# Chunked linear attention into a cosine-gated MLP on one core: pair loading for six chunks instead of four, and two chunks of a pair on two row tiles

## Chip, cores, metric

One core of a Trainium2 chip. The metric is the device time of one execution in microseconds; lower is better.

## What is computed

Per batch (4) and head (8), over 768 time steps with head size 48, a state of 48x48 decays per row and takes up k v^T; the output is q times the state. The outputs of all heads (3072 x 384) go through an MLP with h * cos(h) between two matmuls.

```python
for t in range(S):
    state = alpha[:, :, t, :, None] * state + np.einsum('bhd,bhe->bhde', k[:, :, t], v[:, :, t])
    y[:, :, t] = np.einsum('bhd,bhde->bhe', q[:, :, t], state)
x = y.transpose(0, 2, 1, 3).reshape(B * S, H * D)
h = x @ w_in                      # 384 -> 2048
out = (h * np.cos(h)) @ w_out     # 2048 -> 384
```

## The kernel before

Time is cut into 24 chunks of 128 rows, six for each batch; chunks 2g and 2g+1 are pair g. Within a chunk the recurrence is matrix work: the logarithms of alpha are summed from the chunk's start by a triangular matmul, k is divided and q multiplied by the exponentials of the sums, and then scores (k q), a causal mask, scores times v, and the state of the chunk before times q give the outputs. The state is carried from chunk to chunk with its decay.

For the first SG pairs (two before) a load brings two neighbouring time rows of a head together, 384 bytes in a run instead of 192: partition p holds rows 2p and 2p+1 of the 256 rows of the pair. A buffer then holds the even rows, another the odd rows, of both chunks, the first chunk on partitions 0 to 63 and the second on 64 to 127. Sums, masks and matmuls have forms of their own for that (`sup`, or `j // 2 < SG`).

The order of all work is written out in the string ORDER. Each word is a letter for a unit and a number of a chunk, a pair or a part; the units are issued in this order, each onto its engine's queue, and every engine works its queue strictly in that order. The letters:

- a k q v: loads on SP's queue (L192 to L202). w0 w1: halves of the first MLP matrix, w2 w3: of the second, from POOL's queue (L204 to L214). D: transpose by DMA, o: store of 128 rows, both on SP.
- l: logarithm (ACT, L226), C: sums (TensorE, L234 to L249), E: exponentials (ACT, L255 and L256).
- K and B: k scaled on POOL or DVE (L260); R and O: q scaled on POOL or DVE (L266); P: v cast (POOL, L270); M: decay factors (POOL, L274).
- T, t: transposes on TensorE and their copy (DVE, L286). A, m: scores and mask (L300 or L306, DVE L311). S, u, b: state, its sum with the state before (DVE, L346, or L336 for a first chunk) and its decay (POOL, L336).
- Y, y: outputs of one chunk and their copy out of PSUM (DVE, L406); Q, z: the same for a pair (L385, DVE L425).
- H, h, g: 4 of 16 column blocks of the first MLP matmul for a pair (24 matmuls, L445), its cosine (ACT, L453), the gate (DVE, L458). H0 to H3 belong to pair 0, H4 to H7 to pair 1. H4i and H4i+1 use w0, the others w1. V, e: a quarter of the second MLP matmul of a chunk (4 matmuls, L468; V0 to V3 is chunk 0, the first two quarters use w2, the others w3), and the copy of the finished rows (ACT, L472).
- x: dummy matmuls on a zeroed tile (L481), as many as the number says.

PSUM is handed out by `Slots`: three slots `two` of two banks (for C, A, Q, H) and two slots `one` of one bank (for T, S, Y and the rows of V). A slot that is given back (by E, m, z, g, t, u, y, e) goes to the unit that next takes one in ORDER, which then waits for that reader. SBUF buffers go round by number: four of alpha, three each of k, q and v pairs.

## Time and profile before

| | us |
|---|---|
| median of 5 runs (181.39 to 181.69) | 181.41 |
| the profiled execution | 181.39 |
| its span, first to last instruction | 179.62 |
| what lies around the span (difference) | 1.77 |
| TensorE busy in the span | 172.0 |
| DVE, ACT, POOL busy | 121.8, 111.5, 78.4 |
| end of the last matmul | 175.80 |
| copy of the last rows on ACT (L472) | 0.49 |

The span runs from the first to the last instruction of the program; times in the views count from its start. An engine's busy time is the union of its instructions' times. "idle before" names how long an engine stood before an instruction, and what released it. The chain of waits goes back from the last instruction, at each step to what released it or to the instruction ahead of it on its engine. q1 is the DMA queue of SP, q0 that of POOL; a queue's share is the time that its packets took over that of 16 engines, which passes 100% where an engine has more than one packet under way.

### The profile page before, as it was taken

The page shows a single profiled execution, that of the slowest core. Times are in us where ns is not written, and L with a number is a line of the kernel's source. Part 1 is how long each engine was busy: PE and PEld are TensorE (multiplying, and loading weights), DVE is VectorE, ACT ScalarE, POOL GpSimd, SP SyncE. Part 2 cuts the span into 40 slices and gives each one's busy share as a digit, 9 for nine tenths or more (in the row PEclk, how much of TensorE's full clock was granted, in tenths as well). Part 3 has the DMA queues.
Part 4 walks back from the last instruction along what each step waited for, and adds up shares of the span by engine and source line. Part 5 has one row for each costly group of instructions (what it writes and reads, how often), then busy time and mean ns, then how long its engine had stood idle before and what let it go on. Part 6 is the DMA issues. An engine that isn't in the chain of part 4 may idle for free.

```text
span 179.6 us, 5251 instructions
## 1 busy us (share of the span) xinstructions
PE 172.0 (96%) x2227; PEld 125.9 (70%) x2227; DVE 121.8 (68%) x152; ACT 111.5 (62%) x124; POOL 78.4 (44%) x133
## 2 busy tenths in 40 slices
PE   7978799999999999999999999999999999999991
PEld 2455688866787587876787866875788757788660
DVE  6178898957359688465987596368787679755620
ACT  3544345864778598866869895797765521455431
POOL 7259710223689127952129337952187804100100
PEclk9999999999999999999999999999999999999999
DMA  6999999999999997999999999999819993010112
GB/s 157 325 293 178 199 191 185 186 190 218 215 212 134 204 235 169 198 143 207 222 219 205 222 212 190 158 259 236 190 47 219 211 115 135 0 43 6 46 44 88
DMA packets 113719, 31.01 MB, mean 173 GB/s; under 512 B 107808, under 2 KB 112928, under 8 KB 113696
## 3 DMA queue, kind: packets, MB, share of 16 engines
q1 hardware_dynamic: 110816, 27.53, 75.4%
q0 software_dynamic: 2880, 3.15, 10.7%
q8 instruction: 17, 0.28, 0.6%
q14 instruction: 6, 0.05, 0.1%
HBM read 25.17 MB, written 4.72 MB: 166 GB/s over the span
## 4 chain that ended last, share of the span: by engine, by line
PE 87%; SPq 4%; DMA 3%; DVE 2%; POOL 2%; issue 1%; ACT 0%; POOLq 0%
PE one L468 36%; PE two L445 35%; PE two L385 5%; SPq L197 3%; PE two L306 3%; DMA k_sb<-in_k_dram 3%; PE one L331 2%; PE two L245 2%; PE one L281 2%; PE one L385 1%; PE two L247 1%; DVE qkT L286 1%; SPq L201 1%; POOL kqb L260 1%; POOL vpb L270 1%
## 5 line engine op out<-in xcount | busy, mean ns | idle before, releaser
L458 DVE TENSOR_TENSOR g_sb<-two,c_sb 128x1024 bf16<-128x1024 f32 x48 | 58.2, 1221 | 26.1 <-ACT c_sb L453 25.4
L453 ACT ACTIVATE c_sb<-two,halfpi 128x1024 bf16<-128x1024 f32 x48 | 52.8, 1113 | 32.5 <-PE two L445 30.9
L468 PE MATMUL one<-w,g_sb 128*128 128x384 bf16 x384 | 69.7, 326 | 0.0
L445 PE MATMUL two<-xT,w 128*128 128x256 bf16 x576 | 68.3, 273 | 0.0
L445 PEld LDWEIGHTS <-w 128*128 128x128 bf16 x576 | 55.1, 98 | 8.2
L468 PEld LDWEIGHTS <-g_sb 128*128 128x128 bf16 x384 | 35.9, 98 | 20.9
L260 POOL TENSOR_TENSOR kqb<-k_sb,icp 128x384 bf16<-128x384 f32 x21 | 20.9, 1000 | 26.2 <-DMA k_sb<-in_k_dram 13.6
L336 POOL TENSOR_TENSOR ub<-sc,Em 128x384 bf16<-128x384 f32 x20 | 16.6, 830 | 34.3 <-DVE sc L346 34.2
L311 DVE TENSOR_TENSOR A_sb<-two,mask_f 128x1024 bf16<-128x1024 f32 x20 | 23.5, 1217 | 2.6 <-PE two L306 2.5
L270 POOL CAST vpb<-v_sb 128x384 bf16<-128x384 f32 x24 | 12.2, 514 | 24.3 <-DMA v_sb<-in_v_dram 24.3
L266 POOL TENSOR_TENSOR kqb<-q_sb,cp 128x384 bf16<-128x384 f32 x20 | 19.9, 1000 | 6.0 <-DMA q_sb<-in_q_dram 4.8
L472 ACT ACTIVATE o_sb<-one 128x384 f32<-128x384 f32 x24 | 11.7, 489 | 16.1 <-PE one L468 15.3
L255 ACT ACTIVATE icp<-two 128x768 f32<-128x768 f32 x12 | 9.7, 810 | 11.7 <-PE two L247 8.3
L425 DVE CAST xT<-two 128x768 bf16<-128x768 f32 x10 | 9.6, 956 | 6.2 <-PE two L385 6.2
L346 DVE TENSOR_TENSOR sc<-one,ub 128x384 f32<-128x384 f32 x20 | 11.0, 551 | 3.7 <-PE one L331 3.6
L226 ACT ACTIVATE lnab<-a_sb 128x768 bf16<-128x768 f32 x12 | 10.1, 844 | 3.5 <-DMA a_sb<-in_alpha_dram 2.2
L481 PE MATMUL one<-warm 128*128 128x512 bf16 x31 | 9.6, 452 | 2.4 <-DVE warm L106 1.2
L220 ACT ACT_TABLE_LOAD x8 | 10.3, 1283 | 0.9 <-PEq L510 0.7
L451 ACT ACT_TABLE_LOAD x8 | 10.3, 1283 | 0.1
L286 DVE COPY qkT<-one 128x1024 bf16<-128x1024 bf16 x9 | 6.1, 687 | 5.8 <-PE one L281 3.5
L256 ACT ACTIVATE cp<-two 128x776 f32<-128x776 f32 x12 | 9.7, 812 | 0.0
L385 PEld LDWEIGHTS <-vpb 128*32 128x32 bf16 (+1 forms) x448 | 8.9, 95 | 1.1 <-issue 0.7
(65 smaller groups left out, 120.8 us busy)
## 6 DMA issues: line engine op xcount, KB each, us to landing
out_dram<-o_sb SPq DMA_DIRECT2D x24, 192.0 KB, 2.9
a_sb<-in_alpha_dram SPq DMA_DIRECT2D x20, 192.0 KB, 3.9
k_sb<-in_k_dram SPq DMA_DIRECT2D x20, 192.0 KB, 3.9
q_sb<-in_q_dram SPq DMA_DIRECT2D x20, 192.0 KB, 4.0
v_sb<-in_v_dram SPq DMA_DIRECT2D x20, 192.0 KB, 3.8
w<-in_moe_w_in_dram POOLq DMA_DIRECT2D x2, 768.0 KB, 9.1
w<-in_moe_w_out_dram POOLq DMA_DIRECT2D x2, 768.0 KB, 15.3
a_sb<-in_alpha_dram SPq DMA_DIRECT2D x2, 384.0 KB, 4.1
```

Source lines behind the costliest of these rows:

```text
L260: eng.tensor_tensor(out=kqb[j % 4][:, 0, :, 0:D], in0=slot(k_t, j), in1=icp_t[j // 2 % 3][:, j % 2].rearrange("s (h d) -> s h d", h=H), op ...
L266: eng.tensor_tensor(out=kqb[j % 4][:, 1, :, 0:D], in0=slot(q_t, j), in1=cp.rearrange("s (h d) -> s h d", h=H), op=ALU.mult)
L270: nc.gpsimd.tensor_copy(out=vpb[j % 4][:, :, 0:D], in_=slot(v_t, j))
L311: nc.vector.tensor_tensor(out=A_t[j % 4].rearrange("s (h t) -> s h t", h=H), in0=two[("A", j)].rearrange("s (h t) -> s h t", h=H), in1=(ma ...
L336: eng.tensor_tensor(out=ub[j % 3][:, :, 0:96].rearrange("r p (a e) -> r p a e", a=2), in0=src.rearrange("r p (a e) -> r p a e", a=2), in1= ...
L346: nc.vector.tensor_tensor(out=sc_t[j % 3], in0=t, in1=ub[(j - 1) % 3][:, :, 0:96], op=ALU.add)
L385: nc.tensor.matmul(t[32 * c : 32 * c + 32, kt * C : (kt + 1) * C], lhsT, rhs, start=start, stop=stop, skip_group_check=True)
L445: nc.tensor.matmul(t[:, m * n : (m + 1) * n], w1[:, kk, f * C : (f + 1) * C], x_t[g % 3][:, kk, bs].rearrange("r b t -> r (b t)"), start=( ...
L453: nc.scalar.activation(out=c_s.take((name, i)), in_=two[(name, i)], func=AF.Sin, bias=halfpi, scale=1.0)
L458: nc.vector.tensor_tensor(out=g_t[g % 3][:, fs, bs], in0=shaped(two[(name, i)], name), in1=shaped(c_s[(name, i)], name), op=ALU.mult)
L468: nc.tensor.matmul(one[("o", j)][:, 0:DM], g_t[j // 2 % 3][:, f, j % 2], w2[:, f], start=(f == 0), stop=(f == NF - 1))
L472: nc.scalar.activation(out=o_s.take(j), in_=one[("o", j)][:, 0:DM], func=AF.Copy)
```

## The change

Three pairs instead of two are loaded in the paired form (SG = 3), so that all six chunks of the first batch are. The decay sums of a paired pair are formed by matmuls of two columns for both chunks at once, and their exponentials are taken by an instruction of their own. A new unit N makes the states of both chunks of a pair: its matmuls alternate between partitions 0 to 63 and 64 to 127, and write two PSUM slots. The outputs of a paired pair are always made for both chunks together by Q, again with alternating halves; the unit Y is not used any more. A new unit n copies the last 128 rows out of PSUM half on ACT and half on DVE. ORDER is written anew throughout. Of its 30 rows, the first six and the last of each are shown.

```diff
--- before.py
+++ after.py
@@ -15,32 +15,32 @@
 
 
 ORDER = """
-a0 l0 x9 C0 E0 q0 k0 a2 O0 O1 B1 l1 v0 v2 a5 x10 C1 K0 P0 P3 M1 k2 x1 T1 a4 E1 q2 T0 t0 t1 x6 A0
-K3 A1 w0 M0 P1 P2 B2 m0 m1 l2 R3 x4 S1 S0 u0 k4 q4 u1 C2 Y1 O2 E2 a7 k5 a6 q5 Y0 y1 x1 T2 w1 y0 w2
-b1 R4 M2 S2 t2 T3 u2 t3 S3 A2 B4 b2 A3 H1 v4 w3 v5 T4 a9 a8 v6 k6 q6 q7 m3 m2 h1 u3 v7 t4 H0 h0 Y3
-Y2 g1 H2 M3 h2 H3 h3 y2 g0 y3 g2 H6 h6 g3 g6 K5 H5 k8 k7 M4 q8 H4 h5 H7 V4 V5 V0 h4 V1 h7 P4 b3 l3
-V2 V3 V6 V7 e0 g5 g4 g7 O5 T5 e1 t5 C3 E3 V8 S4 u4 A4 A5 b4 P5 V9 V10 R6 K6 V11 V12 e2 l4 m5 m4 o2
-o0 Q2 z2 C4 S5 V13 k9 q9 M6 P6 M5 K7 u5 R7 P7 M7 H9 T6 V14 E4 h9 V15 a11 a12 t6 S6 H8 e3 g9 b5 u6
...
-u23 h47 g46 V92 V88 V93 g47 o19 o20 o21 V94 V89 V95 V90 e23 o23 V91 e22 b23 o22
+a0 l0 k0 x9 C0 v0 a2 q0 E0 K0 B1 P0 P1 l1 M0 v2 q2 k2 O0 x14 N0 R1 P2 C1 E1 a4 w0 u0 a7 q4 k4 u1
+M1 K2 w1 l2 R3 T0 t0 T1 t1 O2 w2 P3 b1 w3 M2 x4 A1 A0 T2 C2 m1 m0 B3 Q0 t2 E2 T3 a6 a8 t3 a9 z0 x3
+A3 A2 N1 H1 m3 u2 m2 h1 M4 b2 H0 Q1 u3 h0 g1 z1 g0 R5 R4 K5 M3 H3 K4 b3 H2 h3 g3 h2 H6 h6 H4 g2 g6
+V4 H5 H7 V0 V5 V1 v4 v7 q7 h4 h7 h5 g4 g7 g5 V2 V6 P4 P5 V3 e0 V7 e1 o0 T5 V8 V9 t5 T4 V10 t4 V11
+k6 q6 v6 k7 a10 l3 e2 l4 A4 A5 N2 m4 C3 C4 u4 P7 m5 V12 b4 V13 E3 Q2 M6 R6 E4 V14 B6 u5 P6 R7 z2
+a12 k9 q9 B7 o2 D6 V15 S6 H8 u6 e3 h8 S7 a11 q8 K9 M7 R9 T7 u7 H10 k8 D9 k10 a13 h10 g8 H9 k11 v9
...
+V93 o19 V91 V94 V95 b23 e22 o22 n23 o23
 """
 
 
@@ -88,7 +88,7 @@
 
 
 
-    SG = 2
+    SG = 3
     HC = C // 2
 
     sb = ctx.enter_context(tc.tile_pool(name="sb", bufs=1))
@@ -233,12 +233,11 @@
                 for ii in range(2):
                     nc.tensor.matmul(t[:, i, 0:HD], strict2 if ii > i else incl2,
                                      l[:, ii, :, 0:D], start=(ii == 0), stop=(ii == 1))
-            for c in range(2):
-                for p in range(NP):
-                    for i in range(2):
-                        nc.tensor.matmul(t[:, c, HD + p : HD + p + 1],
-                                         l[:, i, 2 * p : 2 * p + 2].rearrange("s h d -> s (h d)"),
-                                         halves[:, c : c + 1], start=(i == 0), stop=(i == 1))
+            for p in range(NP):
+                for i in range(2):
+                    nc.tensor.matmul(t[:, 0, HD + 2 * p : HD + 2 * p + 2],
+                                     l[:, i, 2 * p : 2 * p + 2].rearrange("s h d -> s (h d)"),
+                                     halves, start=(i == 0), stop=(i == 1))
             return
         for i in range(n):
             l = lnab[j // 2 % 2][:, (j + i) % 2]
@@ -253,7 +252,13 @@
         t = two[("c", j)].rearrange("s (i x) -> s i x", i=2)
         g, s = j // 2 % 3, slice(j % 2, j % 2 + n)
         nc.scalar.activation(out=icp_t[g][:, s], in_=t[:, 0:n, 0:HD], func=AF.Exp, scale=-1.0)
-        nc.scalar.activation(out=cp_t[g][:, s], in_=t[:, 0:n, 0:CW], func=AF.Exp, scale=1.0)
+        if j // 2 < SG:
+            nc.scalar.activation(out=cp_t[g][:, s, 0:HD], in_=t[:, 0:n, 0:HD], func=AF.Exp, scale=1.0)
+            nc.scalar.activation(out=cp_t[g][:, s, HD:CW],
+                                 in_=t[:, 0, HD : HD + 2 * NP].rearrange("r (p c) -> r c p", c=2),
+                                 func=AF.Exp, scale=1.0)
+        else:
+            nc.scalar.activation(out=cp_t[g][:, s], in_=t[:, 0:n, 0:CW], func=AF.Exp, scale=1.0)
         two.give(("c", j))
 
     def scale_k(eng, j):
@@ -317,20 +322,23 @@
 
     def state(j):
         t = one.take(("S", j))
-        if j // 2 < SG:
-            r = slice(HC * (j % 2), HC * (j % 2) + HC)
-            for p in range(NP):
-                for i in range(2):
-                    b = (j // 2 * 2 + i) % 4
-                    nc.tensor.matmul(t[:, p * 96 : (p + 1) * 96],
-                                     kqb[b][r, 0, 2 * p : 2 * p + 2].rearrange("s h d -> s (h d)"),
-                                     vpb[b][r, 2 * p : 2 * p + 2, 0:D],
-                                     start=(i == 0), stop=(i == 1))
-            return
         for p in range(NP):
             nc.tensor.matmul(t[:, p * 96 : (p + 1) * 96],
                              kqb[j % 4][:, 0, 2 * p : 2 * p + 2].rearrange("s h d -> s (h d)"),
                              vpb[j % 4][:, 2 * p : 2 * p + 2, 0:D], start=True, stop=True)
+
+
+    def states(g):
+        t = [one.take(("S", 2 * g + c)) for c in range(2)]
+        for p in range(NP):
+            for i in range(2):
+                b = (2 * g + i) % 4
+                for c in range(2):
+                    r = slice(HC * c, HC * c + HC)
+                    nc.tensor.matmul(t[c][:, p * 96 : (p + 1) * 96],
+                                     kqb[b][r, 0, 2 * p : 2 * p + 2].rearrange("s h d -> s (h d)"),
+                                     vpb[b][r, 2 * p : 2 * p + 2, 0:D],
+                                     start=(i == 0), stop=(i == 1), skip_group_check=True)
 
     def decayed(eng, j, src):
         eng.tensor_tensor(
@@ -349,7 +357,7 @@
 
 
 
-    def outputs(j, t):
+    def outputs(j):
         U = ub[(j - 1) % 3].rearrange("r p e -> r (p e)")
         sup = j // 2 < SG
 
@@ -377,14 +385,6 @@
                                 A_t[b][s, ACOL[h] * C : (ACOL[h] + 1) * C]))
             return mms
 
-        def issue(streams):
-            for i in range(max(map(len, streams))):
-                for c, stream in enumerate(streams):
-                    if i < len(stream):
-                        kt, lhsT, rhs, start, stop = stream[i]
-                        nc.tensor.matmul(t[32 * c : 32 * c + 32, kt * C : (kt + 1) * C], lhsT, rhs,
-                                         start=start, stop=stop, skip_group_check=True)
-
 
 
         states, rest = [[] for _ in range(4)], [[] for _ in range(4)]
@@ -393,26 +393,36 @@
             for x, mm in enumerate(a + b):
                 m = (g // 4,) + mm + (g < 4 and x == 0, x == len(a + b) - 1)
                 (states if sup and x < len(a) else rest)[g % 4].append(m)
-        if sup:
-            issue(states)
-        issue(rest)
+        return states, rest
+
+    def issue(*lists):
+        for i in range(max(len(stream) for _, streams in lists for stream in streams)):
+            for c in range(4):
+                for t, streams in lists:
+                    if i < len(streams[c]):
+                        kt, lhsT, rhs, start, stop = streams[c][i]
+                        nc.tensor.matmul(t[32 * c : 32 * c + 32, kt * C : (kt + 1) * C], lhsT, rhs,
+                                         start=start, stop=stop, skip_group_check=True)
 
     def outputs_one(j):
-        outputs(j, one.take(("y", j)))
+        issue((one.take(("y", j)), outputs(j)[1]))
 
     def ev_outputs_one(j):
-        x, t = x_t[j // 2 % 3][:, :, j % 2], one[("y", j)][:, 0 : 3 * C]
-        if j // 2 < SG:
-            nc.vector.tensor_copy(out=x.rearrange("r k (p i) -> r k i p", i=2),
-                                  in_=t.rearrange("r (k i p) -> r k i p", k=3, i=2))
-        else:
-            nc.vector.tensor_copy(out=x, in_=t.rearrange("r (k t) -> r k t", k=3))
+        nc.vector.tensor_copy(out=x_t[j // 2 % 3][:, :, j % 2],
+                              in_=one[("y", j)][:, 0 : 3 * C].rearrange("r (k t) -> r k t", k=3))
         one.give(("y", j))
 
     def outputs_two(g):
         t = two.take(("y", g))
-        for i in range(2):
-            outputs(2 * g + i, t[:, 512 * i : 512 * (i + 1)])
+        t = [t[:, 512 * i : 512 * (i + 1)] for i in range(2)]
+        states, rest = zip(*(outputs(2 * g + i) for i in range(2)))
+
+        if g < SG:
+            issue(*zip(t, states))
+            issue(*zip(t, rest))
+        else:
+            for x in zip(t, rest):
+                issue(x)
 
     def ev_outputs_two(g):
         t = two[("y", g)].rearrange("r (b x) -> r b x", b=2)[:, :, 0 : 3 * C]
@@ -472,6 +482,13 @@
         nc.scalar.activation(out=o_s.take(j), in_=one[("o", j)][:, 0:DM], func=AF.Copy)
         one.give(("o", j))
 
+
+    def ev_last(j):
+        o, n = o_s.take(j), DM // 2
+        nc.scalar.activation(out=o[:, 0:n], in_=one[("o", j)][:, 0:n], func=AF.Copy)
+        nc.vector.tensor_copy(out=o[:, n:DM], in_=one[("o", j)][:, n:DM])
+        one.give(("o", j))
+
     def store(j):
         nc.sync.dma_start(out=out[j * C : (j + 1) * C, :], in_=o_s[j])
         o_s.give(j)
@@ -486,12 +503,12 @@
         "K": lambda j: scale_k(nc.gpsimd, j), "B": lambda j: scale_k(nc.vector, j), "R": lambda j: scale_q(nc.gpsimd, j), "O": lambda j: scale_q(nc.vector, j),
         "P": cast_v, "M": decay,
         "T": transposes, "t": ev_transposes, "D": dma_transposes,
-        "S": state, "u": ev_state, "b": lambda j: decayed(nc.gpsimd, j, sc_t[j % 3]),
+        "S": state, "N": states, "u": ev_state, "b": lambda j: decayed(nc.gpsimd, j, sc_t[j % 3]),
         "A": scores, "m": mask_scores,
         "Y": outputs_one, "y": ev_outputs_one, "Q": outputs_two, "z": ev_outputs_two,
         "F": lambda i: first("F", i), "f": lambda i: act("F", i), "p": lambda i: gate("F", i),
         "H": lambda i: first("H", i), "h": lambda i: act("H", i), "g": lambda i: gate("H", i),
-        "V": second, "e": ev_second, "o": store, "x": warmup,
+        "V": second, "e": ev_second, "n": ev_last, "o": store, "x": warmup,
     }
     for u in ORDER.split():
         units[u[0]](int(u[1:]))
```

## Prediction

> **What bounds the kernel now.** I read four views, in this order: the page's busy shares, TensorE's waits, the chain of waits over the first 23 us, and the DMA queues in three windows.
>
> ```profile
> PE 172.0 (96%) x2227; PEld 125.9 (70%) x2227; DVE 121.8 (68%) x152; ACT 111.5 (62%) x124; POOL 78.4 (44%) x133
> ```
>
> TensorE is busy for 172.0 of 179.6 us, but 9.6 us of that are the 31 dummy matmuls of L481. All that it waits for is this:
>
> ```profile
> PE one L481 <- DVE warm L106: 1.2, 1, 1.2
> PE one L481 <- DVE qkT L286: 0.8, 1, 0.8
> PE one L385 <- DVE ub L336: 0.6, 1, 0.6
> PE one L481 <- DVE xT L406: 0.4, 1, 0.4
> PE two L300 <- DVE qkT L286: 0.3, 1, 0.3
> ```
>
> Every one lies before 22 us. In the timeline TensorE stands at H1 (the first MLP matmul) at 22.4 us and then runs without a gap to 175.8 us. So the end is the time of H1, plus the TensorE work queued from there, plus 3.8 us of tail (175.84 to 179.62). A change gains by an earlier start, less work after it, or a shorter tail, and loses by any wait behind H1.
>
> What sets the start is in the chain:
>
> ```profile
> 6.55 1.15 SPq L201
> 7.75 4.62 DMA k_sb<-in_k_dram
> 12.49 1.00 POOL kqb L260
> 13.50 0.86 POOL w L208
> ...
> 22.48 0.54 PE two L445 x4
> ```
>
> SP issues one load per 1.19 us; the eighth (k of chunks 2 and 3) lands at 12.36; K3 waits for it on POOL, and behind K3 in POOL's queue stands w0, the first weight DMA. The DMA queues (packets, MB, share of 16 engines) in 2.4 to 9.4, 17 to 25 and 25.5 to 35.5 us:
>
> ```profile
> q1 hardware_dynamic: 5915, 2.24, 115.7%
> ```
> ```profile
> q0 software_dynamic: 711, 1.40, 93.6%
> q1 hardware_dynamic: 848, 0.16, 17.3%
> ```
> ```profile
> q0 software_dynamic: 1918, 1.46, 92.9%
> q1 hardware_dynamic: 1922, 0.36, 33.5%
> ```
>
> Before the weights come, q1 (SP's loads) alone fills the engines: 845 packets per us, and a load is 1024 packets whether of one chunk or of two, so about 1.2 us each. Once the weights (q0) flow, the two queues take turns packet by packet, and SP's loads fall to 106, then 192 packets per us. The weight stream is one unbroken run: first packet 15.11 us (1.68 us after w0's issue began at 13.43), last at 36.93. Its four DMAs land at 21.67, 26.32, 32.27 and 37.25; their users H1, H2, V4 and V2 run at 22.4, about 27.3 or later, 35.1 and 37.7. The cover is only 0.5 to 0.8 us for the first and the last. An earlier H1 alone is therefore worth less than 1 us: the weights would be late next.
>
> **What the Trainium skill says.** "DMA: Bandwidth & Descriptors", Specifications: transfers reach line rate from 512 B on. The trace agrees in effect: 384 B packets go at 845 per us, 192 B ones (9.5 to 12 us, 2734 in 2.5 us) at 1094, so twice the bytes cost 1.3 times the time. Its section on queues, rings and completion order: an engine goes round robin over its queues at packet granularity; 1918 against 1922 packets above is that. "TensorEngine Tiling (Array Packing)", Key Properties and Gotcha 1: tiles of different rows run in parallel, a change of mode drains the array, and two row tiles can't use one PSUM bank at once. No row of before shows two row tiles of these matmuls together, but the mode drain is there: four V matmuls take 0.65 us, and 0.76 behind a tiled group. "TensorE: Matmul & The Clock Gate", Part 1: an idle window of about 3.4 us halves the clock; the trace shows 1.00 throughout, with 1.2 us as the longest wait.
>
> **The change, part by part** (durations from the timeline's starts).
> - *TensorE work.* States: 16 matmuls of L325 for two chunks take 0.63 us, 40 ns each; N does the same 16 on two row tiles in two banks: 8 x 42 = 0.34, saving 0.3 per pair if they overlap, 0 if not. Outputs: Y3 and Y2 take 4 streams of 12 (0.28) and 32 (0.56) matmuls twice, 1.68 us; Q1 needs 24 on full rows (6 x 55 ns) and 64 on eight tiles (8 x 55 ns) plus two drains of 0.1: about 0.97, so -0.7 (bounds -0.8 and 0). Column sums: 8 instead of 16 of 25 ns for the first two pairs (-0.2 each). The third pair's cumulative sum takes 4 instead of 2 of 163 ns: +0.33; its scores, states and outputs cost the same as plain ones. Of all this only Q1 and (as before) what follows lies behind H1. Dummies: 30 instead of 31.
> - *ACT and DVE.* Three exps of 128x8 more, about 0.2 each, and one PSUM copy becomes two of 0.53 for the third pair. Both engines wait for TensorE at that place, so I cost them at nothing; uncovered they are 0.8 us.
> - *Loads.* The third pair's four tensors take four DMAs of 1024 packets instead of eight: 4 x 1.2 = 4.8 us less DMA time before 40 us. SP has four issues less.
> - *Order of loads and of w0.* This is what counts. SP now issues a0 k0 v0 a2 q0 v2 q2 k2 a4. At 1.19 us per load they land at 4.15, 5.34, 6.5, 7.8, 9.0, 10.2, 11.4, 12.5, 13.7. On POOL w0 now stands behind K0 P0 P1 M0 R1 P2 and not behind K3. Walk: C0 ends 0.2 sooner, icp 6.7 to 7.5; K0 7.7 to 8.65 (0.95 each); P0, P1 to 9.6; M0 9.75; R1 to 10.7; P2 (v2 has landed) to 11.15; w0 issues at 11.15 instead of 13.43, 2.3 us sooner. w1 (behind K2), w2 and w3 come at about 13.5, 15.3 and 17.6, well before the stream needs them. So the stream shifts by 2.3 us: landings 19.4, 24.0, 30.0 and 35.0; q4 and k4, now 384 B packets, are in its turns and cost it some 5 ns per packet, 0.3 us by w2's end: 30.3 and 35.4.
> - *TensorE's walk.* N0 at 9.65 (P1), C1 to 10.9, T0 and T1 to 11.8, A1 and A0 12.8 to 13.3 (t1 on DVE), C2 when a4 and l2 are done: a4's last packet is due at 13.0, just as the stream starts (11.15 + 1.68 = 12.8), so I give it 0.8 us of delay: landing 14.5, C2 15.4 to 16.3. m0 ends 15.65; Q0 16.3 to 17.0; T3, t3 18.3, z0 19.35; N1 is done by then. H1 at 19.45, against w0 at 19.4. H0, Q1 (m2 22.2) to 23.1; H3 waits for w1 to 24.0; H3 H2 H6 H4 take 5.2; V4 waits from 29.3 for w2, 30.3; V4 H5 H7 V0 V5 V1 take 0.65 + 2.6 + 1.95 = 5.2; V2 at 35.5. Before, V2 stood at 37.75 with the same units done: a lead of 2.25 us. It is set by the weights: row-tile savings, the exps, and up to 1 us of delay of a4 are hidden in the two waits of 0.9 and 1.0 us, and no wait is long enough for the clock.
> - *Behind V2.* Loads after the stream: k4 lands at 35.3, v4 at about 39.1, P5 40.1; T5 at 38, T4 at 39.8 and N2 at 42.4 find them. New here: V7 T5 V8, where before C3 stood between T5 and V8; V8's bank is given back by e1 0.65 us after V7's end, T5 covers 0.45: 0.25 us lost. N2 takes both banks at once and waits for e2, 0.1 to 0.2. C4 and V12 queue behind it. Further on the number of changes between plain and tiled groups is 39 in both orders; I allow 0.1 for waits.
> - *Tail.* ACT's 0.49 us copy of the last rows becomes two halves side by side; ACT's rows of 384 and 1024 elements (0.49, 1.11) give 0.30 for 192, DVE about 0.35. SP's store waits for the later: -0.14.
>
> Sum: -2.25 + 0.25 + 0.15 + 0.1 - 0.14 = -1.9 to -2.0. The profiled execution took 181.39 us (span 179.62 and 1.77 around it), the median is 181.41: 179.4.
>
> **Rivals.**
> - *Given back (180.5).* The loads behind the stream come later than I walk them; K5, P5 or b4 stall TensorE between 36 and 47 us by 1 us more. For: m4, u4, b4, Q2 follow each other with 0.1 us of slack. Against: DMA has 4.8 us less to do.
> - *Hidden anyway (181.3).* The row tiles don't overlap and mode drains grow: by the walk that is +1.4 us ahead of H3, almost all within the waits for weights; by itself it makes no more than 0.5. It needs a later stall too.
> - *Slower (185).* The weights overtake a4. a4's last packet is due at 13.04, w0's first at 12.8. Before, q1 got some 260 to 330 packets through in the stream's first 0.5 us, then nearly none for 1 us, then 87 per us. If w0 starts at 12.0, 900 packets are left, some 640 are trapped for 7.4 us, a4 lands near 22, C2 holds back Q0 behind it, H1 is at 27 and V2 at 41: +3.5. It decides once a4 lands after 19.2, about 400 trapped packets. Against: P2 can't run before v2 lands at 10.2, so w0's first packet isn't before 12.5.
>
> **How the numbers follow.** The forecast (gain 1.4 to 2.9) has 0.62; given back (0.4 to 1.4) 0.13; a gain over 2.9 (the stream itself shorter, by fewer competing packets) 0.05; no difference 0.08; slower 0.12. 0.2% is 0.36 us, about what a measurement of this kernel can tell. Faster 0.80, same 0.08, slower 0.12. Low 178.3 (3.1 gained), high 181.3: these leave out slower and most of no change.
>
> **What would show it.** Right: w0's issue near 11.2 us and landing near 19.4, waits of TensorE for w before H3 and V4, V2 near 35.5. Wrong: a wait of ACT's ln for a_sb beyond 16 us, TensorE waits over 0.5 us behind 40 us, or w landing as before.

## The result, and the profile after

| | before | after |
|---|---|---|
| median, us (executions) | 181.6 (78) | 182.66 (41) |
| the profiled execution | 181.39 | 182.28 |
| its span | 179.62 | 180.32 |

Time after over time before is 1.0033, with a 95% interval of 1.0016 to 1.005: slower by a third of a per cent, where 179.4 us was forecast. Ratios and means compare undisturbed executions with those of the kernel before; the medians hold all of them, and in experiments 2 and 9 most were disturbed.

A part of this lies outside the span. What lies around the span was 1.77 us in the profiled execution before and 1.96 in the one after. In the 42 listed executions of the changed kernel it is 1.7 to 3.1 (median 2.05); in 191 of the kernel before, run beside the experiments, 1.72 to 1.85. The mean span is 180.35 against 180.14, the mean of what lies around it 2.09 against 1.78: about 0.3 of the 0.6 us that the ratio stands for, and the two profiled executions, 0.70 apart, overstate the difference of the spans. The lost clock told of below does not set the two kernels apart: 7 of 42 and 29 of 191 executions have a mean clock of 0.991 or less.

The two spans are cut at three events that both have: H1 (the first MLP matmul), V2 (the first user of w3) and the end of the last matmul, in the two profiled executions. Of each stretch the view gives its bounds, its length, busy time and instructions of each engine, TensorE's clock, and the DMA share and rate. Before:

```profile
0.00:22.41 22.41, 18.65 (x285) 10.82 (x286) 14.63 (x43) 9.54 (x11) 14.93 (x37) 1.00 1.04 230
22.41:37.73 15.32, 15.32 (x215) 12.56 (x209) 14.09 (x14) 10.17 (x9) 1.67 (x4) 1.00 1.22 191
37.73:175.80 138.07, 138.07 (x1736) 102.52 (x1733) 93.08 (x95) 91.30 (x104) 61.85 (x93) 1.00 0.82 163
175.80:179.62 3.82, 0.01 (x1) 0.00 (x0) 0.00 (x0) 0.49 (x1) 0.00 (x0) 1.00 0.28 103
```

After:

```profile
0.00:20.04 20.04, 17.07 (x270) 9.52 (x271) 13.36 (x41) 9.84 (x14) 14.93 (x37) 1.00 1.02 247
20.04:36.59 16.55, 14.47 (x205) 11.74 (x201) 11.56 (x13) 8.43 (x8) 5.68 (x7) 1.00 1.20 202
36.59:175.96 139.37, 139.32 (x1799) 103.27 (x1797) 95.83 (x100) 93.17 (x105) 59.72 (x90) 1.00 0.78 160
175.96:180.32 4.36, 0.00 (x0) 0.00 (x0) 0.36 (x1) 0.33 (x1) 0.00 (x0) 0.82 0.25 90
```

Stretch by stretch: -2.37, +1.23, +1.30, +0.54, together +0.70. H1 did move forward. Half of that is lost before V2, although TensorE has 0.85 us less to do there (14.47 against 15.32): 2.08 us of the stretch are idle. The rest, and more, is lost to more TensorE work behind V2 and to a longer tail. (V2 is found by counting: the stretch of V matmuls that starts at 34.64 has twelve of 163 ns ahead of it; before, sixteen from 35.13.)

TensorE's waits after:

```profile
PE two L404 <- issue: 2.1, 1, 2.1
PE one L498 <- DVE warm L106: 1.2, 1, 1.2
PE two L234 <- ACT lnab L226: 0.6, 2, 0.4
PE one L286 <- POOL kqb L265: 0.5, 1, 0.5
PE two L305 <- issue: 0.4, 1, 0.4
```

No wait for weights is among them, though two of about 1 us were forecast. The largest is new: "issue", so no engine and no transfer that the view knows released it. It stands in the middle of Q1, between the 33rd and 34th of its 64 score matmuls (timeline of TensorE):

```profile
20.04 2.79 PE L455 MATMUL two<-xT,w 128*128 128x256 bf16 x24
22.77 0.53 PE L404 MATMUL two<-qkT,ub 128*32 128x128 bf16 x24
23.23 0.47 PE L404 MATMUL two<-A_sb,vpb 64*32 64x128 bf16 x33
25.77 0.41 PE L404 MATMUL two<-A_sb,vpb 64*32 64x128 bf16 x31 [2.08 <-issue]
26.12 5.42 PE L455 MATMUL two<-xT,w 128*128 128x256 bf16 x48
```

What ran just ahead of 25.77 on the DMA queues is a packet of q8, the queue that carries the program itself (q8's traffic within the span is 17 packets, 0.28 MB, so 16 KB each). In 23.5 to 24.5 us:

```profile
q0 software_dynamic: 165, 0.13, 80.8%
q1 hardware_dynamic: 165, 0.06, 36.0%
q8 instruction: 1, 0.02, 5.9%
```

This packet ran from 23.54 to 24.48, and TensorE went on 1.3 us later. The Trainium skill ("Runtime: NRT & Kernel Launch", Instruction fetch mechanics) says that an engine's program is refilled in blocks of 16 KiB, 256 instructions, by a DMA queue of its own, and calls the cost mostly hidden. The size agrees with the trace (4,536 matmuls and weight loads make 17.7 such blocks); "hidden" does not.

The places of the holes say the same. Of TensorE's matmuls and weight loads, in order of their starts, 446 stand ahead of the 0.4 us hole in A3, and 702 ahead of the hole in Q1: 256 more. The traces of the changed kernel and of eleven experiments have 18 such holes of 0.38 us or more, ahead of H1 and in Q1. They stand behind 444 or 446 and behind 700 or 702 instructions (some records are missing), 256 apart in all six traces with both, whatever unit is at that place; and each ends 1.2 to 1.5 us after the end of a packet of q8.

Taken as the starts of blocks, which is inferred, these places show how the hole comes about. TensorE works off the block that begins at 19.03 by 23.69, in 4.7 us. The packet of the next block starts 4.5 us after 19.03, takes 0.94, and TensorE goes on 1.3 later: 25.77. Before, at the same place of the count, the block takes from 19.1 to 26.15, 7.0 us, and the packet, 3.0 us after its start, ends 3.1 us ahead of the need. So the hole comes as much from the shorter time that the new forms and order need for 256 instructions as from a later packet. (Further on, packets come up to 3 us ahead of starts counted in this way, so the count serves only up to Q1.)

The weights, landing times in us:

| | w0 | w1 | w2 | w3 | w0 to w3 |
|---|---|---|---|---|---|
| before | 21.67 | 26.32 | 32.27 | 37.25 | 15.58 |
| after | 19.67 | 24.07 | 30.65 | 36.19 | 16.52 |
| forecast | 19.4 | 24.0 | 30.3 | 35.4 | 16.0 |

The lead of 2.0 us shrinks to 1.06. The queues in 25.5 to 28.5 us, before:

```profile
q0 software_dynamic: 573, 0.44, 93.6%
q1 hardware_dynamic: 567, 0.11, 33.2%
```

After:

```profile
q0 software_dynamic: 528, 0.41, 86.1%
q1 hardware_dynamic: 529, 0.20, 38.9%
```

The queues still take turns, packet for packet, but q1's packets are now the pairs' 384 bytes, and the weights (q0) get 8% fewer turns in the same time.

One correction to the text ahead: a unit H has 12 matmuls (four blocks of three), with 12 weight loads, not 24 matmuls.

### The profile page after: what moved, and what is told of

It is laid out like the page before. It is cut to its first block, busy times and chain, and to the rows that moved or that the text cites. A ratio compares the mean times of both kernels' runs of the same rounds, so it can differ in the third digit from the quotient of the medians.

```text
span 180.3 us, 5337 instructions
## 1 busy us (share of the span) xinstructions
PE 170.9 (95%) x2268; PEld 124.5 (69%) x2268; DVE 121.1 (67%) x153; ACT 111.8 (62%) x127; POOL 80.3 (45%) x134
## 4 chain that ended last, share of the span: by engine, by line
PE 87%; SPq 5%; DMA 3%; issue 2%; ACT 1%; DVE 1%; ACTq 0%
PE one L478 35%; PE two L455 35%; PE two L404 6%; SPq L197 5%; PE two L311 3%; DMA a_sb<-in_alpha_dram 3%; PE one L326 2%; PE two L244 2%; PE one L286 2%; PE two L305 1%; PE two L246 1%; PE one L338 1%; ACT lnab L226 0%; PE two L234 0%; DVE qkT L291 0%
## 5 line engine op out<-in xcount | busy, mean ns | idle before, releaser
L271 POOL TENSOR_TENSOR kqb<-q_sb,cp 128x384 bf16<-128x384 f32 x22 | 22.2, 1016 | 17.9 <-DMA q_sb<-in_q_dram 13.6
L316 DVE TENSOR_TENSOR A_sb<-two,mask_f 128x1024 bf16<-128x1024 f32 x18 | 21.3, 1216 | 1.4 <-PE two L311 1.4
L482 ACT ACTIVATE o_sb<-one 128x384 f32<-128x384 f32 x23 | 11.2, 489 | 13.4 <-PE one L478 11.7
L435 DVE CAST xT<-two 128x768 bf16<-128x768 f32 x9 | 8.6, 958 | 5.4 <-PE two L404 5.4
L404 PE MATMUL two<-A_sb,vpb 128*32 128x128 bf16 (+1 forms) x480 | 10.1, 220 | 2.1 <-issue 2.1
L404 PEld LDWEIGHTS <-vpb 128*32 128x32 bf16 (+1 forms) x480 | 8.2, 94 | 3.2 <-issue 2.8
L498 PE MATMUL one<-warm 128*128 128x512 bf16 x30 | 8.8, 447 | 1.4 <-DVE warm L106 1.2
```

The costliest lines, as they stand in the source:

```text
L271: eng.tensor_tensor(out=kqb[j % 4][:, 1, :, 0:D], in0=slot(q_t, j), in1=cp.rearrange("s (h d) -> s h d", h=H), op=ALU.mult)
L316: nc.vector.tensor_tensor(out=A_t[j % 4].rearrange("s (h t) -> s h t", h=H), in0=two[("A", j)].rearrange("s (h t) -> s h t", h=H), in1=(ma ...
L404: nc.tensor.matmul(t[32 * c : 32 * c + 32, kt * C : (kt + 1) * C], lhsT, rhs, start=start, stop=stop, skip_group_check=True)
L482: nc.scalar.activation(out=o_s.take(j), in_=one[("o", j)][:, 0:DM], func=AF.Copy)
```

## Experiments

All ratios are to the kernel before, also where an expectation speaks of the changed kernel, whose own ratio is 1.0033.

Two theories stood after the result. A: the weight stream sets the start, and pair packets slowed it. B: TensorE's own chain sets it, through the hole in Q1. For the time behind V2, the third pair's forms and the tail were suspected.

**1. The weights later.**

```diff
-k2 O0 x14 N0 R1 P2 C1 E1 a4 w0 u0 a7 q4 k4 u1
-M1 K2 w1 l2 R3
+k2 O0 x14 N0 R1 P2 C1 E1 a4 u0 a7 q4 k4 u1
+M1 K2 w0 w1 l2 R3
```

> The changed kernel with w0 behind K2 on POOL, as the kernel before had it behind K3. Theory: the weight stream sets V2. w0 issues near 14.0 instead of 11.2, its first packet at 15.7; w3 lands near 38.5 instead of 36.2, V2 stands there, 2 us later, and the time rises by 1.6 to 2.2 us. Rival: TensorE's own chain (a4, C2, Q0, z0) sets V2, and then less than 0.7 us is lost; a4 lands sooner, near 13.8.

Median 185.04 (four executions), ratio 1.017 [1.0123, 1.0217]; span 183.9. w0 landed at 23.04, w3 at 38.13, V2 stood at 40.19. Waits of TensorE:

```profile
PE two L455 <- DMA w<-in_moe_w_in_dram: 3.5, 1, 3.5
```

So the early place of w0 is needed. But the loss is more than the shift, and V2 came 2.06 us behind w3: in the two windows of 3.41 us behind that wait TensorE's clock was halved (column before the last two):

```profile
18.72:22.13 3.41, 0.89 (x48) 0.65 (x36) 3.41 (x6) 0.17 (x1) 2.32 (x6) 1.00 1.13 202
22.13:25.54 3.41, 2.45 (x12) 1.77 (x13) 0.46 (x1) 0.00 (x0) 3.41 (x5) 0.50 1.12 200
25.54:28.96 3.42, 3.42 (x38) 2.26 (x36) 1.23 (x1) 1.65 (x2) 1.19 (x2) 0.50 1.24 184
```

**2. The kernel before, with its weights sooner** (w0 ahead of K3).

```diff
-C1 K0 P0 P3 M1 k2 x1 T1 a4 E1 q2 T0 t0 t1 x6 A0
-K3 A1 w0 M0
+C1 K0 P0 P3 M1 w0 k2 x1 T1 a4 E1 q2 T0 t0 t1 x6 A0
+K3 A1 M0
```

> The kernel before with w0 ahead of K3 on POOL, nothing else. w0 issues near 11.1 instead of 13.4. Theory: there H1 was held by the loads and not by w, and a5, k2, q2 now share the engines with the stream: q2 (10th load, 8 chunks' worth queued behind 12.5 us) is trapped behind weight packets, T2 and all behind it come some us later: slower by 2 to 6 us. Rival: only the start of the weights counted, and the kernel gains 0.5 us or more.

Ratio 1.0009 [0.9976, 1.0041], median 185.4, span 181.0. w0 landed at 19.49, as wanted, but H1 stayed at 22.50 and V2 came at 39.14: q4, caught in the stream, landed at 24.12, and T4 stood 1.1 us for POOL's scaled q. Moving the weights is worth nothing by itself here; the loads ahead of the stream must be arranged for it.

**3. No weights while Q1's block is fetched** (w1 to w3 behind b2).

```diff
-M1 K2 w1 l2 R3 T0 t0 T1 t1 O2 w2 P3 b1 w3 M2
+M1 K2 l2 R3 T0 t0 T1 t1 O2 P3 b1 M2
-A3 A2 N1 H1 m3 u2 m2 h1 M4 b2 H0
+A3 A2 N1 H1 m3 u2 m2 h1 M4 b2 w1 w2 w3 H0
```

> The changed kernel with w1, w2 and w3 issued only behind b2 on POOL (near 22 us), so that no weight packets flow between w0's end (about 18.5) and 23.5. Fetch theory: the third 16 KB block of TensorE's program, asked for near 19.3 us, then starts to load within 1 us of that and not 4 us later, and Q1 runs without a hole (1.0 to 1.2 us instead of 3.35). Rival (the hole is a wait on data or a bank): the hole stays, near 2 us. On the end: w1 lands near 29 and H3 waits for it, w3 near 42, V2 there: 5 us slower or more by either theory, more where the idle clock halves.

190.66 us, span 188.9: TensorE waited 7.0 us for w1, and the time says no more than that. The hole says it all:

```profile
24.11 0.73 PE L404 MATMUL two<-A_sb,vpb 64*32 64x128 bf16 x64
31.88 2.52 PE L455 MATMUL two<-xT,w 128*128 128x256 bf16 x11 [7.03 <-DMA w<-in_moe_w_in_dram]
```

All 64 score matmuls of Q1 run through in 0.73 us. By the count above the block began at 19.92, and the next packet started at 21.55, after w0 had landed (20.84): 1.6 us behind, not 4.5. The block before began at 14.03, and its successor's packet, among w0's, came 3.7 us behind; the hole in A3 that goes with it is there, 0.8 us long. So the hole is a program fetch that the weight stream holds up.

**4. Q1 behind H3**, to spread its many short instructions.

```diff
-H0 Q1 u3 h0 g1 z1 g0 R5 R4 K5 M3 H3 K4
+H0 u3 h0 g1 g0 R5 R4 K5 M3 H3 Q1 z1 K4
```

> The changed kernel with Q1 and its copy z1 behind H3 instead of ahead of it. Theory: the 2.1 us hole in Q1 is TensorE out of instructions, because the fetch of its next 16 KB of program is held up by the weight stream; with H3 (24 instructions in 1.3 us) and its wait for w1 ahead of Q1, the block has come by then, and the hole shrinks to under 0.5 us. V2 then stands at w3's landing, about 36.2 instead of 36.6, so the time falls by only 0.3 to 0.4 us. Rival: the hole is a wait of Q1 on its mask or state (m2, b2), and has gone or not for that reason: then Q1 would wait at its first matmul, not at its 34th of 64. Rival 2: the hole was the whole loss; then the time falls by 2 us.

Ratio 1.0086 [1.0063, 1.011], median 183.61: the wrong way. The profiled execution is the longest of 22 (186.05, span 183.2). The hole is gone, but TensorE now comes to H3 at 23.4 and waits 2.84 us for w1 (landed 26.17). Then the clock falls:

```profile
22.91:26.32 3.41, 0.57 (x6) 0.28 (x4) 2.54 (x3) 1.43 (x2) 0.00 (x0) 1.00 1.22 203
26.32:29.73 3.41, 3.41 (x52) 2.18 (x59) 0.00 (x0) 0.79 (x1) 1.32 (x2) 0.50 1.25 204
```

**5. Half the weights.** w1 and w3 are not loaded; their users read w0 and w2. This kernel leaves out half of both matrices and repeats the other half.

```diff
-M1 K2 w1 l2 R3 T0 t0 T1 t1 O2 w2 P3 b1 w3 M2
+M1 K2 l2 R3 T0 t0 T1 t1 O2 w2 P3 b1 M2
-w1[:, kk, f * C : (f + 1) * C]
+w1[:, kk, f % 8 * C : (f % 8 + 1) * C]
-w2[:, f]
+w2[:, f % 8]
```

> The changed kernel with the weight DMAs w1 and w3 left out; their users read w0 and w2 in their place, so the output is that of an MLP with repeated halves. It takes half of the weight stream away. Theory (the stream's end sets V2, the hole in Q1 comes from the stream): w2 lands near 25.5, H3 follows Q1 with no wait, the third block of TensorE's program still comes late because w2 flows at 20 us, and so V2 stands between 34.4 (no hole) and 35.6 (1 us of hole), against 36.6: 1 to 2.2 us faster than the changed kernel. Rival: V2 is set by TensorE's own chain and the hole; V2 stays at 36.4 or later and the time within 0.4 us.

Ratio 1.0063 [1.0031, 1.0094], median 183.91, span 182.0: with half the bytes it is slower, not 1 to 2 us faster. The hole is as long as ever (w2 flows at the time of the fetch, which ran at 23.66), and here it halves the clock:

```profile
22.50:25.91 3.41, 1.52 (x64) 0.98 (x61) 1.77 (x3) 1.62 (x2) 1.67 (x2) 1.00 1.25 212
25.91:29.32 3.41, 3.22 (x44) 2.27 (x45) 2.16 (x3) 0.00 (x0) 2.72 (x5) 0.50 0.96 202
```

V2 stood at about 38.4, though the last weights landed at 26.60. Theory A alone is out: TensorE's own chain with its hole holds V2 as well as the weights do.

**6. Two pairs in the paired form, as before**, with the rest of the change kept.

```diff
-    SG = 3
+    SG = 2
-E1 a4 w0 u0 a7 q4 k4 u1
+E1 a4 a5 w0 u0 a7 q4 q5 k4 k5 u1
-V5 V1 v4 v7 q7
+V5 V1 v4 v5 v7 q7
-A4 A5 N2 m4
+A4 A5 S4 S5 m4
```

> The changed kernel with two pairs in the paired form instead of three: chunks 4 and 5 come by eight loads, a5 behind a4, and are computed in the plain form. Theory: a5 becomes the tenth load and is trapped behind the weight packets, which flow from 13.8: it lands between 18 and 26 us instead of a4's 14.1, C2 waits for it with Q0 behind it, and H1 starts at 23 to 30: 3 us slower or more. In return w2 and w3 pass faster (192-byte packets in their turns): 11 us for both instead of 12.1, and Q2 takes 0.90 instead of 1.13. Rival: the third pair was no help, and this kernel is as fast as the changed one or faster by Q2's and C3's 0.4 us.

Ratio 1.0012 [0.999, 1.0035], median 181.74, span 179.9. My theory said that a fifth alpha load ahead of the weights would be caught in them; a5 landed at 14.35, and nothing was lost. The third paired pair is no help: without it the stream is quicker (w3 at 35.46), Q2 starts 0.32 us and ends 0.55 sooner (46.43 to 47.32, after: 46.75 to 47.87). But at V20, 8 us on, the lead is down to 0.05 (55.16, 55.21). By ratio this is not apart from the changed kernel's 1.0033. What is apart is the time around the span: 1.73 to 1.82 us here, and at most 1.85 in every kernel with two paired pairs, while the changed kernel and experiments 1, 4, 5, 7 and 10, all with three, reach 2.1 to 3.1 (experiment 3, also with three, has a single execution, 1.8).

**7. Row tiles undone** (the two chunks of N and Q one after the other; of the edit, the part in Q is shown).

```diff
-            issue(*zip(t, states))
-            issue(*zip(t, rest))
+            for i in range(2):
+                issue((t[i], states[i]))
+                issue((t[i], rest[i]))
```

> The changed kernel with the two chunks of a pair one after the other in N and Q (same instructions, not interleaved), so that no two row tiles can overlap. If the tiles do overlap in the changed kernel: N1 0.63 instead of 0.45 us, Q0 and Q2 longer by 0.5 to 0.6. Theory: the weights set V2, so that what lies ahead of V2 (N0, Q0, N1, Q1) costs less than 0.5 us there, and N2 and Q2 behind it cost their full 0.7: together 0.7 to 1.2 us slower. Rival: the overlap is worth its full sum of about 2.3 us. Rival 2: the tiles don't overlap, and nothing changes.

Ratio 1.0131 [1.0088, 1.0175] (four executions), median 183.37, span 181.1. By the ratio row tiles are worth about 1% here, by the profiled spans 0.7 us. The units' times, from start to start, say directly that the tiles overlap: Q2 takes 1.68 us here and 1.13 in the changed kernel, N1 0.63 and 0.45.

Against the kernel before, Q0 gains much less. There Y1 and Y0 stand next to each other without matmuls of another form between them, and their score matmuls overlapped already: 64 took 0.94 us (before), as against 0.63 for 32 in Y3 or Y2, and 0.73 for 64 in Q0 (after).

```profile
17.52 0.94 PE L385 MATMUL one<-A_sb,vpb 64*32 64x128 bf16 x64
```
```profile
16.33 0.73 PE L404 MATMUL two<-A_sb,vpb 64*32 64x128 bf16 x64
```

**8. Row tiles alone, on the kernel before**: Q0 for Y1 and Y0, Q1 for Y3 and Y2.

```diff
-C2 Y1 O2 E2 a7 k5 a6 q5 Y0 y1 x1 T2 w1 y0 w2
+C2 Q0 O2 E2 a7 k5 a6 q5 z0 x1 T2 w1 w2
-H0 h0 Y3
-Y2 g1 H2
+H0 h0
+Q1 g1 z1 H2
```

> The kernel before with one part of the change: its outputs of pairs 0 and 1 are made for both chunks at once on two row tiles (Q0 for Y1 and Y0, Q1 for Y3 and Y2); loads, states, order and tail are as before. Theory: Q1 takes about 1.1 instead of 1.68 us, T2 waits for no slot, H1 starts 0.3 to 0.5 sooner; V2 can't start before w3 at 37.25, and stood at 37.73: 0.3 to 0.5 us faster than before, ratio about 0.998. Rival: H2 or H3 waits for a PSUM slot that Q1 now holds, and the gain is gone (ratio 1.000 or more). Rival 2: the whole 0.9 us is gained.

Ratio 1.0017 [0.9989, 1.0046], median 182.64, span 179.9. What the row tiles save, TensorE spends waiting for weights, which also came later here (w3 at 37.98 against 37.25):

```profile
PE two L447 <- DMA w<-in_moe_w_in_dram: 0.9, 1, 0.9
PE one L470 <- DMA w<-in_moe_w_out_dram: 0.2, 1, 0.2
```

Q1 has no hole in it here: its 64 matmuls take 0.74 us.

**9. Row tiles, and w0 ahead of K3**, T4 put behind V7 (both edits above together).

> The kernel before with row-tile outputs of pairs 0 and 1, w0 ahead of K3 on POOL, and T4 moved from between H1 and H0 to behind V7. Theory: the weights come 1 us sooner than in the kernel before (w3 near 36.6), T4 no longer waits for q4 behind them, TensorE is ready for V2 at about 36.2, so V2 stands at 36.6 to 36.8 and V7's and T4's end at 39.8 against 40.34: 0.4 to 0.6 us faster than before. Rival: the waits for w1 and w3 make idle windows, the clock halves for 3.4 us in many executions, and the median is 1 us slower.

Median 186.32 (six executions), span 180.7; no ratio is on record. Two executions, 182.09 and 182.52, stand near the kernel before (mean 182.03), four at 185.3 to 188.5 with mean clocks of 0.986 to 0.991. The forecast gain is in none of them. A lower clock is what the rival had, but there is no trace of such an execution, so its reason is not shown. In the profiled one (182.52) no window of 3.41 us runs below 1.00, and TensorE waits not for weights but for POOL's decayed state (0.8) and for DVE (0.6, 0.5): the next limits are close behind.

**10. The last rows copied by ACT alone.**

```diff
-b23 e22 o22 n23 o23
+b23 e22 o22 e23 o23
```

> The changed kernel with its last rows copied by ACT alone (e23 for n23), all else equal. Theory: ACT and DVE read the same PSUM bank, so the DVE half (0.36 us) starts only when the ACT half (0.33) has ended, and the split costs 0.73 where the whole copy takes 0.49: last matmul to last store shorter by 0.25 to 0.3 us, time ratio to the changed kernel about 0.9985. Rival: the longer tail of the changed kernel (4.34 against 3.81 us from the last matmul's end) is the runtime's closing sequence and not the copy; then the tail stays at 4.2 or more.

Ratio 1.0014 [0.9989, 1.0038], median 181.92, span 179.6. One whole copy is shorter than the two halves: the store starts 0.60 us behind the last matmul, not 0.83. The tail is 4.11 us, still 0.3 longer than before; most of that lies behind the store's landing (1.66 against 1.41), so the rival was right in part. The chain of the changed kernel shows why; the halves run one after the other:

```profile
176.04 0.34 ACT o_sb L488
176.38 0.02 issue
176.41 0.36 DVE o_sb L489
```

Here w3 landed at 36.10 and V2 ran at 36.15: with a hole of 1.4 us the weights are the later of the two.

**11. The last rows in two PSUM banks** (on the kernel of experiment 6), columns 0 to 191 in one and the rest in the other.

```diff
+        if j == 23:
+            if qq == 0:
+                two.take(("o", j))
+            for f in range(4 * qq, 4 * qq + 4):
+                for x in range(2):
+                    nc.tensor.matmul(two[("o", j)][:, 512 * x : 512 * x + DM // 2], g_t[j // 2 % 3][:, f, j % 2],
+                                     w2[:, f, DM // 2 * x : DM // 2 * (x + 1)], start=(f == 0), stop=(f == NF - 1))
+            return
```

> The changed kernel with two paired pairs, and the last 128 rows accumulated in two PSUM banks: columns 0 to 191 in one, 192 to 383 in the other (32 matmuls of 192 columns in place of 16 of 384), read by ACT and by DVE. Theory (the halves followed each other because both lay in one bank): DVE's half starts with ACT's, within 0.1 us, and the store starts 0.50 to 0.55 us behind the last matmul, against 0.83 with both halves in one bank and 0.6 with one whole copy; the narrower matmuls cost 0 to 0.4 us of TensorE. Median 181.3 to 181.9, ratio 0.995 to 1.000. Rival (something else orders the two halves, such as the output tile that they share): DVE still starts 0.3 us behind ACT, 0.83 us to the store, ratio 1.000 to 1.003.

Ratio 1.0008 [0.9982, 1.0034], span 180.1. The Trainium skill ("PSUM — Partial Sum Buffer", PSUM bank collisions raise a hardware error) has two engines kept apart where they touch one bank, reads included. That was my theory of the tail, and it does not hold: with two banks DVE still starts when ACT is done.

```profile
176.25 0.33 ACT L496 ACTIVATE o_sb<-two 128x192 f32<-128x192 f32 x1 [0.83 <-PE two L480]
176.61 0.36 DVE L497 COPY o_sb<-two 128x192 f32<-128x192 f32 x1 [3.28 <-ACT o_sb L496]
```

**12. The same two banks as two tiles** of the program.

```diff
-                two.take(("o", j))
+                two.take(("o", j)); two.take(("o2", j))
-two[("o", j)][:, 512 * x : 512 * x + DM // 2]
+two[(("o", "o2")[x], j)][:, 0 : DM // 2]
-in_=two[("o", j)][:, 512 : 512 + n]
+in_=two[("o2", j)][:, 0:n]
```

> As the kernel with the last rows in two PSUM banks, but the two banks are now two tiles of the program (two slots, each giving one of its banks) instead of the two halves of one tile. With one tile the program makes DVE's half wait for ACT's, whatever the bank; with two tiles DVE's instruction waits for TensorE alone. Theory (that wait of the program is the whole reason why the halves follow each other): DVE starts within 0.1 us of ACT, and the store begins 0.45 to 0.55 us behind the last matmul, against 0.83 with one tile and 0.6 with one whole copy; ratio 0.994 to 1.000, about 0.3 us less than with one tile. Rival (the two engines can't read PSUM together here): 0.8 us from the last matmul to the store again, or both halves start together and each takes 0.6 us or more.

Ratio 0.9987 [0.9961, 1.0014], median 181.88, span 179.4.

```profile
175.79 0.33 ACT L496 ACTIVATE o_sb<-two 128x192 f32<-128x192 f32 x1 [0.75 <-PE two L480]
175.83 0.36 DVE L497 COPY o_sb<-two 128x192 f32<-128x192 f32 x1 [2.87 <-PE two L480]
```

Now DVE is released by TensorE, not by ACT, and the two reads overlap. From the start of the copy to the store it is 0.46 us, against 0.75 with one tile and 0.52 with one whole copy. So the wait is one that the program sets between two readers of one tile. Whether two readers of one bank could run together was not tried. Done rightly, the split is worth 0.06 us.

**13. Two pairs, and ACT alone for the last rows** (edits 6 and 10 together), the best that these runs point to.

> Two pairs in the paired form (as in the run before), and the last rows copied by ACT alone; all else as in the changed kernel. Theory: the tail gives back 0.25 to 0.3 us, the plain third pair 0.3 us: level with the kernel before or up to 0.3 us faster, ratio 0.998 to 1.000. Rival: the late k5 and q5 stall TensorE near 40 us in most executions, ratio 1.003 or more.

Ratio 0.9976 [0.9949, 1.0003], median 181.88, span 179.3. The gain is at the edge of what the runs can tell. The stream, from w0 (19.50) to w3 (35.07), takes 15.57 us, as before the change, so the third pair's packets lengthened it (by how much is taken up below). At Q2's end this kernel is 1.02 us ahead of the changed one (46.85), at V20 0.36 (54.85). DVE shows where the rest goes:

```profile
48.75 1.03 DVE L265 TENSOR_TENSOR kqb<-k_sb,icp 128x384 bf16<-128x384 f32 x1 [0.76 <-DMA k_sb<-in_k_dram]
49.71 0.55 DVE L344 TENSOR_TENSOR ub<-one,Em 128x384 bf16<-128x384 f32 x1
```

k of chunk 7 lands at 48.73 (after: 46.43), the reader of S6 stands behind its scaling on DVE, and S7 on TensorE waits for that reader.

**14. The same, with k of chunks 6 and 7 loaded sooner.**

```diff
-V5 V1 v4 v5 v7 q7 h4
-k6 q6 v6 k7 a10
+V5 V1 v4 v5 v7 k6 h4
+k7 q6 v6 q7 a10
```

> The kernel with two paired pairs and ACT alone for the last rows, with k of chunks 6 and 7 loaded two places sooner (v4 v5 v7 k6 | k7 q6 v6 q7 in place of v4 v5 v7 q7 | k6 q6 v6 k7). In that kernel TensorE is 1.02 us ahead of the changed kernel when Q2 ends (46.85 against 47.87), and 0.36 ahead at V20 (54.85 against 55.21): DVE's scaling of k7 waits 0.76 for the load (landed 48.73), the first state of the second batch stands behind it on DVE, and S7 on TensorE behind that. Theory (the plain form of the third pair costs less on TensorE, but its eight loads instead of four delay k7, and that is why taking it back gained nothing): k7 lands at 45 to 46.5, DVE doesn't wait, V20 stands at 54.1 to 54.5, span 178.6 to 179.0, ratio 0.992 to 0.996. Rival (another load or POOL's chain is late next, q7 among them, which now lands at about 47.5 and is used at 48.4): V20 at 54.7 to 54.9, span 179.2 to 179.5, ratio 0.996 to 1.000.

Ratio 1.0022 [0.9994, 1.005], median 182.05, span 179.5: no gain. The rival's mechanism was right, though the ratio lies above its range. k7 lands at 46.36 and DVE no longer waits; now v6 (47.62) is late:

```profile
48.97 0.33 PE L326 MATMUL one<-vpb,kqb 128*128 128x96 bf16 x4 [0.49 <-POOL vpb L275]
```

V20 stands at 54.99. With eight plain loads for the third pair one load or another is late near 48 us, and the lead ends there; with four paired ones TensorE never waits, but has more to do. That fits with the third pair's form moving the span so little either way.

## Why the prediction was wrong

Forecast span 177.7 (179.62 - 2.25 + 0.25 + 0.15 + 0.1 - 0.14), measured 180.32: 2.6 us missed, and in every stretch some. The step that failed first is that the walk prices units by their matmuls alone: it has no term for the fetch of TensorE's own program (holes of 0.4 and 2.08 us). Smaller steps failed behind V2, in the tail and around the span.

- **w0's issue: right.** It began at 11.18 (11.15 forecast) and a4 landed at 14.15 (14.5), so the rival in which the weights overtake a4 did not happen. "1.68 us to the first packet" became 2.60 (13.78); w0 still landed only 0.27 late.
- **H1 at 19.45: it ran at 20.04, +0.59**, with w0 there since 19.67. "N1 is done by then" failed: t3's copy was done at 18.36, as forecast, but A3's second matmul came only at 19.03, behind the first program hole, and A2 and N1 followed. Without it N1 would have been done at about 19.4, and H1 would have started at w0's landing, 19.67.
- **"Pair packets cost the stream 0.3 us": mis-sized.** From w0 to w3 it took 16.52 us with pairs, 15.57 in experiment 13 with the third pair plain: 0.95. The size is uncertain, as experiment 10, with the same loads as the changed kernel, has 15.99, and experiment 6 15.83. w3 landed at 36.19, so V2 could not run before that, 0.7 later than forecast.
- **"Two waits of 0.9 and 1.0 us hide the rest": failed.** A 2.08 us hole, which no step foresaw, took the place of both waits. Without it TensorE would have been at V4 about 2 us sooner and waited for w2 until 30.65 (it ran V4 at 31.37), then for w3; so the hole's own cost at V2 is some 0.4 us (36.59 against 36.19). Experiment 5 has the hole holding V2 without the weights, experiment 10 (a hole of 1.4 us) the weights holding it.
- **"V2 with the same units done": wrong.** Before, T4 ran at 23.73, between H1 and H0, ahead of V2. After, it runs at 41.23, behind V7. That is 0.45 us of the work behind V2 that I counted on neither side.
- **V8's wait for e1: right.** T5 took 0.65 instead of 0.45: 0.2, 0.25 forecast.
- **"Scores, states and outputs [of the third pair] cost the same as plain ones": failed.** Start to start: Q2 1.13 us against 0.90, scores 0.57 against 0.55, N2 0.51 against 0.43: 0.33 together (its sums, C2, lie ahead of H1 in both kernels, as the prediction has it). With T4 and T5 that is 0.98 of the 1.30 us in the third stretch. C3, of the fourth pair and plain in both, took 0.67 against 0.53 in its new place; 0.18 are spread over the rest, where I had allowed 0.1. What the form bought is four loads less, which I counted as DMA time and put to no use; experiments 13 and 14 show that plain loads would have cost about as much in waits (0.66 us of lead).
- **Tail: -0.14 became +0.54.** "Two halves side by side" failed: one behind the other, matmul to store 0.83 against 0.55 (+0.28). The other 0.27 lie between the store's landing and the end (1.68 against 1.41). They go with the third paired pair and not with the copy: 1.66 to 1.68 in six of the seven traces with three paired pairs (1.50 in experiment 5), 1.26 to 1.29 in the five of the new order with two. The cause is open.
- **"1.77 around it" taken over as it was: failed.** The changed kernel's median is 2.05. Three profiled executions, all with three paired pairs, have an 18th packet of q8 1.1 to 1.8 us behind the end of the span: the changed kernel (1.96 us around the span) and experiments 4 (2.84) and 10 (1.89). In the traces with 17 packets it is 1.77 to 1.84. With 66 instructions not on record, as the first hole implies (446 + 66 = 512), this program is at least 4,602 long, and 18 blocks hold 4,608; the other kernels are about 80 or more shorter. So a fetch in the closing sequence is likely; no run tests it.

Row tiles overlap as the prediction said, but save less: 0.55 for Q1 (1.68 to the 1.13 that Q2 takes without a hole; 0.7 forecast), 0.18 per pair of states (0.3 forecast), and little for Q0, since Y1 and Y0 overlapped before ("no row of before shows two row tiles together" was wrong). It was right that their saving ahead of the weights is hidden. One more reading was off: the window of 9.5 to 12 us holds 1587 packets of 192 B and 1103 of 384, so 1094 per us is not the rate of 192 B packets alone. The rival nearest to the result was "hidden anyway" (181.3); it needed a later stall, and that was the hole. I gave this side 0.08 and "slower" only to a mechanism that did not occur.

Left open: why a fetch lags 3 to 4.5 us under the weights, what lengthens the time behind the last store's landing and around the span, and how much of the ratio each piece holds, since the intervals of experiments 6, 10, 12, 13 and 14 overlap.

## What to carry to other kernels

An earlier start is worth what all the limits behind it allow: here TensorE's chain with its program fetch, the weights and the loads behind them all stood within 1 us of it, and each took its part. When units change places, list for each stretch what lies on either side of its end, and price every new form of a unit by its own matmuls and drains. A form that does the same number of matmuls in less time also uses up its program sooner. Splitting a copy over two engines needs two tiles, and a look at which engine releases the second half.

## What was not expected of the hardware

- TensorE can run out of program. Where short matmuls go by at two instructions in some 11 to 28 ns (Q1, N1), a block of 256 lasted 4.7 us. By the count of the holes, the next 16 KB packet came 1.0 to 2.4 us behind a block's start where no weights flowed (kernel before, experiments 1, 3, 5 and 8) and 3.0 to 4.5 behind that of the block that begins ahead of H1 where they did (all traces but that of experiment 3). No hole stands in MLP matmuls (24 instructions in 1.31 us).
- The clock halves after a window that is only partly idle. The Trainium skill ("TensorE: Matmul & The Clock Gate", Part 1) speaks of an idle window of about 3.4 us. Here TensorE was busy for 0.57, 0.89 and 1.52 of 3.41 us in the window ahead (experiments 4, 1 and 5), and the next ran at 0.50; in experiment 3 it was 0.85. Windows busy for 1.89 and 1.90 (experiments 13 and 12) kept 1.00. At half clock 2.45 and 2.36 (experiments 1 and 3) were not enough to come back in the next window, 3.22 (experiment 5) was. The changed kernel's hole fell across two windows, the worse one still busy for 1.97, and kept 1.00:

```profile
21.72:25.13 3.41, 1.97 (x68) 1.38 (x65) 2.21 (x3) 2.07 (x2) 0.43 (x1) 1.00 1.19 207
25.13:28.54 3.41, 2.77 (x54) 2.41 (x55) 2.16 (x3) 0.90 (x1) 1.54 (x2) 1.00 1.25 202
```

  So a wait of 2 us costs once as itself, and, where it falls within one window, can cost up to 1.7 us more of lost clock (an estimate: half of 3.41).
